# Fourier mixing after top-k attention on one core: the token tails folded once, on GpSimd, and the row sums' small constant added by ScalarE

## The chip, the cores and the metric

The kernel runs on one core of a Trainium2 chip. The core has a matrix engine (TensorE, PE in the profile; its weight loads are a row of their own, PEld), a vector engine (VectorE, DVE), an activation engine (ScalarE, ACT), a general engine (GpSimd, POOL) and queues that start transfers (SyncE, SP). Each engine works through its own list of instructions in order and waits at semaphores for the others. The metric is the device time of one execution, in microseconds (us), as the median of several runs.

## The reference

There are 8 batches. Each has 8 heads, 576 tokens and 64 channels per head. What is computed, per batch:

```
scores = q k^T / 8                       # 576 x 576 per head
kth    = 32nd largest score of each row
attn   = exp(scores - max) where scores >= kth, else 0
attn   = attn / (row sum + 1e-9)
x      = attn v, heads side by side       # 576 x 512
mixed  = Re FFT over channels (FFT over tokens (x))
u      = x + mixed
un     = (u - mean) / sqrt(var + 1e-6)
out    = u + relu(un w_ch1) w_ch2         # 512 -> 2048 -> 512
```

All of it is float32.

## The kernel before, in words

**Attention.** A batch has 4 pairs of heads, and a pair has 9 items (line 265): four token tiles of 128 rows for each of two heads, and one item for the remaining 64 tokens of both heads. So a batch is 36 items and the kernel 288. The 576 tokens are two halves of 288 = 128 + 128 + 32; tiles 0 and 1 are the first half's full tiles, 2 and 3 the second's, and tile 4 holds the two tails of 32, the first half's in partitions 0 to 31 and the second half's in 32 to 63.

For an item, TensorE makes the scores (lines 298, 313, 328), ScalarE moves them out of PSUM, and VectorE finds the 32 largest with four rounds of `max` and three of `match_replace` (lines 349, 351). GpSimd then makes two bounds per row from them (`bounds`, line 358, tile `nt`), ScalarE a mask term (line 365), GpSimd subtracts it (line 366), ScalarE takes the exponential and sums each row into `den` (line 372), TensorE transposes the result (line 393) and multiplies it with `v` (line 430). `attended` (line 439) copies the product out, moves two pieces of `den`, and leaves on a list for VectorE the function `inverse`: add 1e-9 (line 457), take the reciprocal (line 460), result in `rd`. `to_tokens` (line 465) transposes the product back into rows of tokens and scales it by `rd` into `x` (line 479, or on ScalarE at line 498 for batch 1).

**Fourier mixing.** The transform over tokens uses symmetries so that its matmuls are shorter. First the input is folded. Over tokens: a token and the one 288 later are added (even frequencies, parity 0) or subtracted (odd, parity 1). Over channels: the two halves of the 512 channels are added and subtracted, and within each result mirrored channels are added and subtracted. `fold_ops` (line 519) builds these operations for one batch and parity: `moved` brings the second half's tail down to partitions 0 to 31 (ScalarE, line 546), `first` is the token step (tile `sd`, line 551 for the full tiles and 554 for the tail), `second` the channel halves (tile `zw`, line 560), `third` the mirrored channels in two parts (tile `fg`, lines 569 to 581). Each step has a part for the two full tiles (128 partitions, two slots) and one for the tail (32 partitions, third slot). `dft_tokens` (line 603) then runs 30 matmuls per parity against tables of cosines and sines (line 617): 16 with the full tiles, 6 for one single channel, 8 with the tails. `dft_channels` (line 661) transforms over channels; the sum, the statistics and a reciprocal square root follow, partly on GpSimd (lines 696, 720 to 725), and the result is transposed for the network (line 737).

**Network.** `mlp_units` (line 745) cuts a batch's two matrix products into units: `hidden` (line 759), then `back` (lines 783, 819). They stand in a queue and are used as filler for TensorE.

**Order.** It is written out by hand. The main loop (line 1056) goes through steps; step i works on item i's top-k, on the scores of item i+3 and on the transposes of item i-2. `at(step, where, fn)` (line 889) puts a function at a place in a step: `pe` and its relatives among TensorE's work, `act` on ScalarE after the mask, `pool0` on GpSimd ahead of `bounds(i)`, `pool` after it, `dve` behind the step's top-k on VectorE. How much filler a step takes is settled by a planner from fixed costs (`fixed_cost`, `level`), not from measured times. The loop over batches at line 952 places each batch's folds, transforms and network: batch 0 ends with nothing behind it, and VectorE folds it whole (lines 957 to 966); for batch 1, GpSimd does `first` and `third` of the full tiles and VectorE the rest (lines 967 to 980); batches 2 to 6 are folded on GpSimd (lines 981 to 987); for the last batch VectorE folds parity 0 and GpSimd parity 1 at the same time (lines 988 to 994).

**Buffers.** The pool `batp` has one buffer per tag. `fold_s` holds in turn `sd`, `fg`, the moved mixed values of three tiles, the network's input and its output; `fold_d` holds `zw` and others.

Of the kernel before, what the change touches and what calls it, by code (L numbers as in the profile page):

```python
# [9 lines left out]
F32 = mybir.dt.float32  # L10
# [3 lines left out]
ALU = mybir.AluOpType  # L14
# [4 lines left out]
P = 128  # L19
# [40 lines left out]
def kernel(  # L60
# [378 lines left out]
    def attended(pair, ch, late):  # L439

        o, w = o_of.pop((pair, ch)), CW[ch]
        PT.pop((pair, ch))
        xT = attp.tile([P, CW[0]], F32, name=f"xT_{pair}_{ch}", tag="xT", bufs=4)
        nc.scalar.copy(out=xT[:, 0:w], in_=o[:, 0:w])
        xT_of[pair, ch] = xT
        den = den_t[pair % 3]
        if ch == 0:
            for h in range(2):
                nc.scalar.copy(
                    out=den[TH * h:TH * (h + 1), 5:6],  # L450
                    in_=den[TAIL + TH * h:TAIL + TH * (h + 1), 4:5],
                )
        c0, n = (0, 6) if ch == 0 else (6, 4)
        rd = small.tile([P, 6], F32, name=f"rd_{pair}_{ch}", tag="rd", bufs=6)

        def inverse():
            nc.vector.tensor_scalar(
                out=rd[:, 0:n], in0=den[:, c0:c0 + n], scalar1=1e-9, scalar2=None, op0=ALU.add
            )
# [56 lines left out]
    PARTS = [(slice(0, P), slice(0, 2)), (slice(0, TH), slice(2, 3))]  # L516
    folded, y_of, yt_of, us_of, rs_of, unT_of = ({} for _ in range(6))

    def fold_ops(b, par, eng, space="own", mid=None):

# [4 lines left out]

        def buf(n, name):  # L530
            if space == "hT":
                return sp[:, 3 * DM * n:3 * DM * (n + 1)].rearrange("p (s c) -> p s c", s=3)
            pool, tag = (batp, ("fold_s", "fold_d")) if space == "own" else (attp, ("PT0", "PT1"))
            return pool.tile([P, 3, DM], F32, name=f"{name}_{b}_{par}", tag=tag[n % 2], bufs=1)

        got = folded[b, par] = []

        def place(n):
            while len(got) <= n:
                got.append(buf(len(got), ("sd", "zw", "fg")[len(got)]))  # L540
            return got[n]

        def moved():

            out, in_ = place(0)[0:TH, 2, :], x[TH:TAIL, 4, :]
            nc.scalar.copy(out=out, in_=in_)

        def first(p):
            sd, op = place(0), ALU.add if par == 0 else ALU.subtract
            if p == 0:  # L550
                eng[0].tensor_tensor(out=sd[:, 0:2, :], in0=x[:, 0:2, :], in1=x[:, 2:4, :], op=op)
            else:
                s_ = sd[0:TH, 2, :]
                eng[1].tensor_tensor(out=s_, in0=x[0:TH, 4, :], in1=s_, op=op)

        def second(p):
            pp, ss = PARTS[p]
            s_, z_ = place(0)[pp, ss], place(1)[pp, ss]
            for cols, op in ((slice(0, Q2), ALU.add), (slice(Q2, DM), ALU.subtract)):
                (mid or eng[p]).tensor_tensor(  # L560
                    out=z_[:, :, cols], in0=s_[:, :, 0:Q2], in1=s_[:, :, Q2:DM], op=op
                )

        def third(n, p):
            pp, ss = PARTS[p]
            z_, f_ = place(1)[pp, ss], place(2)[pp, ss]

            def tt(out, up, down, op):
                eng[p].tensor_tensor(out=f_[:, :, out], in0=z_[:, :, up], in1=z_[:, :, down], op=op)

            if n == 0:
                eng[p].memset(f_[:, :, Q1:Q1 + 1], 0.0)
                eng[p].tensor_copy(out=f_[:, :, 0:DM:Q2], in_=z_[:, :, 0:DM:Q2])
                up, down = slice(1, Q1), slice(Q2 - 1, Q1, -1)
                tt(up, up, down, ALU.add)
                tt(slice(Q1 + 1, Q2), up, down, ALU.subtract)
            else:
                up, down = slice(Q2 + 1, Q3), slice(DM - 1, Q3, -1)
                tt(up, up, down, ALU.subtract)
                tt(slice(Q3, DM - 1), up, down, ALU.add)  # L580
                eng[p].tensor_copy(out=f_[:, :, DM - 1:DM], in_=z_[:, :, Q3:Q3 + 1])

        return {"moved": moved, "first": first, "second": second, "third": third}

    def fold_steps(f, moved=True):

        def one():
            if moved:
                f["moved"]()
            f["first"](0)  # L590
            f["first"](1)

        def two():
            f["second"](0)
            f["second"](1)

        def three(n):
            f["third"](n, 0)
            f["third"](n, 1)

        return [one, two, lambda: three(0), lambda: three(1)]

    def dft_tokens(b, par):

        while any(u[2] == "hidden" for u in queue):
            one_unit()
        _, zw, fg = folded[b, par]
        if b not in y_of:
            y_of[b] = batp.tile([P, 4, S], F32, name=f"y_{b}", tag="y")
        y = y_of[b]  # L610
# [17 lines left out]
        for g2 in range(2):  # L628
            for gg in range(2):
                g = 2 * g2 + gg  # L630
                for st in range(2):
# [29 lines left out]
    def dft_channels(b, t, quick=False):  # L661
# [22 lines left out]
        key = (b, t > 1 and t < 4)  # L684
        if key not in us_of:
            us_of[key] = batp.tile(
                [P, 3, DM], F32, name=f"us_{b}_{t}", tag="fold_d" if key[1] else "fold_s"
            )
        us = us_of[key][0:rows, CHUNKS[int(key[1])].index(t), :]
        nc.scalar.copy(out=two(us), in_=mp[0:rows])  # L690
# [261 lines left out]
    for b in range(B):  # L952
# [3 lines left out]
        T0 = end + (2 if first else 3 if soon else 4)  # L956
        if first:

            def folds(b=b, T0=T0):
                for par, space in ((0, "own"), (1, "hT")):  # L960
                    f = fold_ops(b, par, (nc.vector,) * 2, space)
                    at(T0, "act", f["moved"])
                    for op in fold_steps(f, False):
                        at(T0, "dve", op)
            at(T0, "begin", folds)
            ft, fc = (T0 + 1, T0 + 1), T0 + 1
        elif soon:
# [12 lines left out]
            ft, fc = (T0 + 3, T0 + 6), T0 + 7  # L980
        elif not last:
            for par in range(2):
                def folds(par=par, b=b, T0=T0):
                    for n, op in enumerate(fold_steps(fold_ops(b, par, (nc.gpsimd,) * 2))):
                        at(T0 + (6 if par else 1) + n, "pool0", op)
                at(T0, "begin", folds)
            ft, fc = (T0 + 5, T0 + 11), T0 + 12
        else:
            def folds(b=b):
                a = fold_steps(fold_ops(b, 0, (nc.vector,) * 2))  # L990
                for op in a + fold_steps(fold_ops(b, 1, (nc.gpsimd,) * 2, "PT")):
                    op()
            at(T0, "dve", folds)
            ft, fc = (T0 + 1, T0 + 3), T0 + 4
# [207 lines left out]
```

## Time and profile before

The median of three runs is 2008.23 us (2002.4 to 2011.8). The profiled execution spans 2002.2 us at a mean granted TensorE clock of 0.966.

| engine | busy us | share of the span |
|---|---|---|
| TensorE, matmuls | 1856.8 | 93% |
| VectorE | 1639.2 | 82% |
| ScalarE | 1230.1 | 61% |
| GpSimd | 835.0 | 42% |

The groups of instructions that the change touches, by line and shape:

| line, engine, operation | shape | count | busy us | mean ns |
|---|---|---|---|---|
| 457 VectorE, add 1e-9 | 128x4 | 32 | 14.0 | 437 |
| 457 VectorE, add 1e-9 | 128x6 | 32 | 10.6 | 332 |
| 546 ScalarE, move the tail | 32x512 | 15 | 9.2 | 617 |
| 551 GpSimd, token step | 128x1024 | 13 | 31.2 | 2398 |
| 554 GpSimd, token step, tail | 32x512 | 11 | 14.3 | 1302 |
| 560 GpSimd, channel halves | 128x512 | 22 | 28.5 | 1314 |
| 560 GpSimd, channel halves, tail | 32x256 | 22 | 16.1 | 749 |
| 569 GpSimd, mirrored channels | 128x254 | 52 | 37.8 | 749 |
| 569 GpSimd, mirrored channels, tail | 32x127 | 44 | 19.0 | 449 |
| 560 VectorE, channel halves | 128x512 | 8 | 7.2 | 942 |

The page cuts the span into 40 slices of 50 us and gives each engine's busy share in each; it is read first for which engine is full where. An average over the span hides that the first batch, the middle and the end have different limits. A group's busy time counts from an instruction's start to its end, so an instruction that is held up after its start looks long. "Idle before" is the time in which an engine stood still ahead of an instruction, with the instruction that released it.

### The profile page before, as it was taken

The numbers are of one execution on the slowest core, as the hardware profiler recorded it, in microseconds if no ns is written. First come the engines' busy times: TensorE is split into PE (matmuls) and PEld (weight loads), VectorE is DVE, ScalarE is ACT, GpSimd is POOL, SyncE is SP. The second block draws the span as 40 slices with busy tenths as digits, with TensorE's granted clock in tenths as the row PEclk, the third lists the DMA queues.
The fourth block names the chain that finished last, engine by engine and source line by source line (L and its number), as shares of the span: only waits on it lengthen the run. The fifth ranks groups of instructions, "written<-read, shape, count | busy, mean of one in ns | idle before, by whom it ended". The sixth has DMA issues, their size and how long they took to land.

```text
span 2002.2 us, 27534 instructions
## 1 busy us (share of the span) xinstructions
PE 1856.8 (93%) x8626; PEld 1122.8 (56%) x8626; DVE 1639.2 (82%) x3391; ACT 1230.1 (61%) x3047; POOL 835.0 (42%) x1114
## 2 busy tenths in 40 slices
PE   5666589999889999999999999999999999998999
PEld 3333356475555656647565656646565656565655
DVE  7999989999999999988889888888889889843100
ACT  6888747776766767656676667656665667541100
POOL 4878833324433365224632374225533464223000
PEclk9777699999999999999999999999999999998999
DMA  4333100011000100000000001010000101000000
GB/s 123 102 84 100 56 5 19 24 27 31 17 19 24 27 24 24 19 23 21 24 24 18 24 15 29 19 32 19 18 24 24 26 13 30 1 14 1 11 14 11
DMA packets 133585, 57.82 MB, mean 29 GB/s; under 512 B 124352, under 2 KB 124480, under 8 KB 133440
## 3 DMA queue, kind: packets, MB, share of 16 engines
q1 hardware_dynamic: 132208, 55.73, 10.5%
q8 instruction: 69, 1.13, 0.2%
q14 instruction: 76, 0.62, 0.1%
q10 hardware_dynamic: 1232, 0.33, 0.1%
HBM read 46.57 MB, written 9.44 MB: 28 GB/s over the span
## 4 chain that ended last, share of the span: by engine, by line
PE 70%; DVE 12%; issue 6%; ACT 6%; POOL 6%; DMA 0%; POOLq 0%; DVEq 0%; ACTq 0%
PE cp L783 20%; PE hp L759 19%; PE o L430 7%; PE sp L328 5%; PE tpP L393 5%; DVE m L349 5%; DVE wk L351 4%; PE yp L617 3%; POOL wk L366 2%; PE cp L819 2%; PE mp L673 2%; PE sp_t L298 2%; ACT wk L365 1%; ACT wk L372 1%; POOL w L192 1%
## 5 line engine op out<-in xcount | busy, mean ns | idle before, releaser
L366 POOL TENSOR_TENSOR wk<-S,wk 128x576 f32<-128x576 f32 x288 | 409.9, 1423 | 861.8 <-ACT wk L365 814.0
L349 DVE MAX8 m<-wk 128x8 f32<-128x576 f32 x864 | 623.1, 749 | 5.4
L759 PE MATMUL hp<-unT,w 128*128 128x256 f32 (+1 forms) x2048 | 538.0, 409 | 3.7 <-POOL t L721 2.2
L783 PE MATMUL cp<-w,hT 128*128 128x512 f32 x1024 | 478.7, 599 | 0.0
L759 PEld LDWEIGHTS hp<-unT,w 128*128 128x128 f32 x2048 | 372.5, 190 | 128.0 <-issue 32.0
L351 DVE MATCH_REPLACE8 wk<-m,wk 128x576 f32<-128x576 f32 x576 | 427.6, 742 | 0.0
L783 PEld LDWEIGHTS cp<-w,hT 128*128 128x128 f32 x1024 | 179.5, 190 | 183.1 <-issue 182.3
L372 ACT ACTIVATE wk<-wk,nt 128x576 f32<-128x576 f32 x288 | 224.9, 781 | 76.5 <-POOL wk L366 75.1
L393 PE MATMUL tpP<-ident,wk 128*128 128x128 f32 x1152 | 189.0, 289 | 74.7 <-ACT wk L372 39.0
L365 ACT ACTIVATE wk<-S,nt 128x576 f32<-128x576 f32 x288 | 226.2, 785 | 48.2 <-POOL nt L358 46.0
L393 PEld LDWEIGHTS tpP<-ident,wk 128*128 128x128 f32 x1152 | 141.4, 147 | 177.9 <-ACT wk L372 61.3
L349 DVE MAX8 m<-S 128x8 f32<-128x576 f32 x288 | 214.1, 743 | 30.4 <-ACT S L302 29.9
L396 ACT COPY PT<-tpP 128x512 f32<-128x512 f32 (+1 forms) x320 | 171.0, 545 | 109.5 <-PE tpP L393 107.1
L763 ACT ACTIVATE hT<-hp 128x320 f32<-128x320 f32 (+1 forms) x256 | 104.8, 409 | 188.7 <-PE hp L759 186.8
L351 DVE MATCH_REPLACE8 wk<-m,S 128x576 f32<-128x576 f32 x288 | 213.7, 742 | 0.0
L430 PE MATMUL o<-PT,v 128*64 128x256 f32 (+3 forms) x1440 | 194.5, 413 | 4.9 <-ACT PT L396 4.4
L331 ACT COPY S<-sp 128x512 f32<-128x512 f32 (+1 forms) x264 | 141.9, 588 | 73.0 <-PE sp L328 72.7
L328 PE MATMUL sp<-kT,qT 64*128 64x512 f32 (+1 forms) x528 | 166.5, 689 | 2.9 <-ACT means L937 1.9
L430 PEld LDWEIGHTS o<-PT,v 128*64 128x64 f32 x1440 | 110.9, 152 | 78.2 <-issue 15.7
L192 POOL TENSOR_TENSOR w<-w,space 128x512 f32<-128x512 f32 x96 | 123.6, 1287 | 5.3 <-ACT space L183 2.0
L797 DVE SCALAR_TENSOR_TENSOR x<-cp,gi,x 128x512 f32<-128x512 f32 x11 | 8.2, 746 | 128.3 <-PE cp L783 128.3
L298 PEld LDWEIGHTS sp_t<-kt,qT 128*128 128x128 f32 (+1 forms) x322 | 51.7, 188 | 62.6 <-issue 23.8
(123 smaller groups left out, 1874.4 us busy)
## 6 DMA issues: line engine op xcount, KB each, us to landing
space<-in_moe_w_ch_dram SPq DMA_DIRECT2D x32, 512.0 KB, 3.7
nat<-in_q_dram SPq DMA_DIRECT2D x128, 64.0 KB, 2.1
v<-in_v_dram SPq DMA_DIRECT2D x128, 64.0 KB, 2.2
out_dram<-x SPq DMA_DIRECT2D x32, 256.0 KB, 2.1
nat<-in_k_dram SPq DMA_DIRECT2D x124, 64.0 KB, 2.2
nat<-in_q_dram SPq DMA_DIRECT2D x128, 8.0 KB, 1.8
v<-in_v_dram SPq DMA_DIRECT2D x128, 8.0 KB, 1.8
nat<-in_k_dram SPq DMA_DIRECT2D x124, 8.0 KB, 1.7
```

The lines of the kernel that those rows point to most:

```text
L192: nc.gpsimd.tensor_tensor(out=dst, in0=dst, in1=(low, high, ex)[part], op=ALU.mult if part else ALU.add,)
L328: nc.tensor.matmul(sp[r], lhsT=qT[hd, q_cols], rhs=kT[hd, :], start=True, stop=True)
L349: ops.append(lambda src=src, m8=m8: nc.vector.max(out=m8, in_=src))
L351: ops.append(lambda src=src, m8=m8: nc.vector.match_replace(w, m8, src, NEG))
L365: nc.scalar.activation(out=w, in_=Ssb[i], func=AF.Relu, scale=-FAR, bias=Nt[i][:, 1:2])
L366: nc.gpsimd.tensor_tensor(out=w, in0=Ssb.pop(i), in1=w, op=ALU.subtract)
L372: nc.scalar.activation(out=w, in_=w, func=AF.Exp, bias=Nt.pop(i)[:, 0:1], accum_out=den_t[pair % 3][:, c:c + 1],)
L393: nc.tensor.transpose(tp[:, c, :], p_sb[:, k0 + P * c:k0 + P * (c + 1)], ident)
L396: nc.scalar.copy(out=pt[:, NF * he:NF * (he + 1), col:col + w], in_=tp[:, :, o:o + w])
L430: nc.tensor.matmul(o[D * e:D * (e + 1), c0:c1], lhsT=vv[:, c, e, :], rhs=pt[:, 2 * NF if c == NF else NF * e + c, c0:c1], start=(c == 0), ...
L759: nc.tensor.matmul(hp[:, 0:w], lhsT=w1[:, dt, P * it:P * (it + 1)], rhs=unT[:, dt, 0:w], start=(dt == 0), stop=(dt == NDT - 1),)
L783: nc.tensor.matmul(cp, lhsT=hT[:, it, P * n:P * (n + 1)], rhs=w2[:, it, :], start=(it == 0), stop=(it == NIT - 1),)
```

## The change

There are three parts.

1. The tails are no longer folded over tokens. All 64 rows of tile 4 are folded over channels only, once per batch, by GpSimd (`fold_tails`), into a tile of their own (`fold_t`, with one more column for the single channel). Both parities use it: the tables for the tail rows are now made for the tokens' own positions, for 64 rows. `moved` and the tail parts of `first`, `second` and `third` are gone. `fold_tails` is placed one step ahead of the folds (for batch 0 behind the bounds of that step, for the others ahead of them).
2. Batch 1's folds are all on GpSimd: `first` and `second` in one step, both parts of `third` in the next, for each parity.
3. `inverse` is now only the reciprocal on VectorE. ScalarE adds the 1e-9, in `attended`, behind the copies of `den`.

```diff
-            a = 2.0 * np.pi * ((np.outer(P * st + p, kk) % S) / S)
+            tok = P * st + p
+            if st == 2:
+                tok = np.where(p < TH, tok, S // 2 + tok - TH)
+            a = 2.0 * np.pi * ((np.outer(tok, kk) % S) / S)
...
-        def inverse():
-            nc.vector.tensor_scalar(
-                out=rd[:, 0:n], in0=den[:, c0:c0 + n], scalar1=1e-9, scalar2=None, op0=ALU.add
-            )
-            nc.vector.reciprocal(out=rd[:, 0:n], in_=rd[:, 0:n])
-
-        late.append(inverse)
+        nc.scalar.activation(out=rd[:, 0:n], in_=den[:, c0:c0 + n], func=AF.Copy, bias=1e-9)
+        late.append(lambda: nc.vector.reciprocal(out=rd[:, 0:n], in_=rd[:, 0:n]))
...
-    ROWS3 = (P, P, TH)
+    ROWS3 = (P, P, TAIL)
...
+    def fold_tails(b, eng):
+        z = batp.tile([P, DM], F32, name=f"zt_{b}", tag="fold_s")[0:TAIL]
+        ft_of[b] = batp.tile([P, DM + 1], F32, name=f"ft_{b}", tag="fold_t")
+        f = ft_of[b][0:TAIL]
+        fold_halves(eng, x_of[b][0:TAIL, 4, :], z)
+        for n in range(2):
+            fold_channels(eng, z, f[:, 0:DM], n)
+        eng.tensor_copy(out=f[:, DM:DM + 1], in_=z[:, Q1:Q1 + 1])
...
-        for st in range(3):
+        for st in range(2):
             mm(0, 1, st, zw[:, st, Q1:Q1 + 1], 1, 0)
+        mm(0, 1, 2, tails[:, DM:DM + 1], 1, 0)
...
-                mm(g2, gg, 2, fg[:, 2, P * g:P * (g + 1)], P, gg)
+                mm(g2, gg, 2, tails[:, P * g:P * (g + 1)], P, gg)
...
         if first:
-            def folds(b=b, T0=T0):
+            at(T0 - 1, "pool", lambda b=b: fold_tails(b, nc.gpsimd))
+            def folds(b=b):
                 for par, space in ((0, "own"), (1, "hT")):
-                    f = fold_ops(b, par, (nc.vector,) * 2, space)
-                    at(T0, "act", f["moved"])
-                    for op in fold_steps(f, False):
-                        at(T0, "dve", op)
-            at(T0, "begin", folds)
+                    for op in fold_ops(b, par, nc.vector, space):
+                        op()
+            at(T0, "dve", folds)
         elif soon:
+            at(T0 - 1, "pool0", lambda b=b: fold_tails(b, nc.gpsimd))
             for par in range(2):
-                def folds(par=par, b=b, T1=T0 + 1 + 3 * par):
-                    f = fold_ops(b, par, (nc.gpsimd, nc.vector), mid=nc.vector)
-                    at(T1 if par else T1 - 1, "act", f["moved"])
-                    at(T1, "pool0", lambda: f["first"](0))
-                    at(T1, "dve", lambda: [
-                        f["first"](1), f["second"](0), f["second"](1),
-                        f["third"](0, 1), f["third"](1, 1),
-                    ])
-                    at(T1 + 1, "pool0", lambda: [f["third"](n, 0) for n in range(2)])
+                def folds(par=par, b=b, T0=T0):
+                    for n, op in enumerate(fold_ops(b, par, nc.gpsimd)):
+                        at(T0 + 1 + 3 * par + n // 2, "pool0", op)
                 at(T0, "begin", folds)
         elif not last:
+            at(T0, "pool0", lambda b=b: fold_tails(b, nc.gpsimd))
             for par in range(2):
                 def folds(par=par, b=b, T0=T0):
-                    for n, op in enumerate(fold_steps(fold_ops(b, par, (nc.gpsimd,) * 2))):
+                    for n, op in enumerate(fold_ops(b, par, nc.gpsimd)):
                         at(T0 + (6 if par else 1) + n, "pool0", op)
         else:
+            at(T0 - 1, "pool0", lambda b=b: fold_tails(b, nc.gpsimd))
             def folds(b=b):
-                a = fold_steps(fold_ops(b, 0, (nc.vector,) * 2))
-                for op in a + fold_steps(fold_ops(b, 1, (nc.gpsimd,) * 2, "PT")):
+                a = fold_ops(b, 0, nc.vector)
+                for op in a + fold_ops(b, 1, nc.gpsimd, "PT"):
                     op()
```

More of the change, by code (lines that the diff above doesn't have):

```diff
@@ L514, with fold_channels, tt, fold_halves @@
     Q1, Q2, Q3 = DM // 4, DM // 2, 3 * DM // 4
-    ROWS3 = (P, P, TH)
-    PARTS = [(slice(0, P), slice(0, 2)), (slice(0, TH), slice(2, 3))]
-    folded, y_of, yt_of, us_of, rs_of, unT_of = ({} for _ in range(6))
-    def fold_ops(b, par, eng, space="own", mid=None):
+    ROWS3 = (P, P, TAIL)
+    folded, ft_of, y_of, yt_of, us_of, rs_of, unT_of = ({} for _ in range(7))
+    def fold_channels(eng, z, f, n):
+        def tt(out, up, down, op):
+            eng.tensor_tensor(out=f[..., out], in0=z[..., up], in1=z[..., down], op=op)
+        if n == 0:
+            eng.memset(f[..., Q1:Q1 + 1], 0.0)
+            eng.tensor_copy(out=f[..., 0:DM:Q2], in_=z[..., 0:DM:Q2])
+            up, down = slice(1, Q1), slice(Q2 - 1, Q1, -1)
+            tt(up, up, down, ALU.add)
+            tt(slice(Q1 + 1, Q2), up, down, ALU.subtract)
+        else:
+            up, down = slice(Q2 + 1, Q3), slice(DM - 1, Q3, -1)
+            tt(up, up, down, ALU.subtract)
+            tt(slice(Q3, DM - 1), up, down, ALU.add)
+            eng.tensor_copy(out=f[..., DM - 1:DM], in_=z[..., Q3:Q3 + 1])
+    def fold_halves(eng, s_, z):
+        for cols, op in ((slice(0, Q2), ALU.add), (slice(Q2, DM), ALU.subtract)):
+            eng.tensor_tensor(out=z[..., cols], in0=s_[..., 0:Q2], in1=s_[..., Q2:DM], op=op)
+    def fold_tails(b, eng):
[6 more added lines that the diff above has]
+        eng.tensor_copy(out=f[:, DM:DM + 1], in_=z[:, Q1:Q1 + 1])
+    def fold_ops(b, par, eng, space="own"):
         x = x_of[b]
@@ L531, in buf @@
             if space == "hT":
-                return sp[:, 3 * DM * n:3 * DM * (n + 1)].rearrange("p (s c) -> p s c", s=3)
+                return sp[:, 2 * DM * n:2 * DM * (n + 1)].rearrange("p (s c) -> p s c", s=2)
             pool, tag = (batp, ("fold_s", "fold_d")) if space == "own" else (attp, ("PT0", "PT1"))
-            return pool.tile([P, 3, DM], F32, name=f"{name}_{b}_{par}", tag=tag[n % 2], bufs=1)
+            return pool.tile([P, 2, DM], F32, name=f"{name}_{b}_{par}", tag=tag[n % 2], bufs=1)
@@ L536, in fold_ops @@
         got = folded[b, par] = []
[L538 to L569, printed above, removed]
-            if n == 0:
[L572 to L601, printed above, removed]
+        def first():
+            got.append(buf(0, "sd"))
+            op = ALU.add if par == 0 else ALU.subtract
+            eng.tensor_tensor(out=got[0], in0=x[:, 0:2, :], in1=x[:, 2:4, :], op=op)
@@ L603, in dft_tokens, with second, third @@
+        def second():
+            got.append(buf(1, "zw"))
+            fold_halves(eng, got[0], got[1])
+        def third(n):
+            if n == 0:
+                got.append(buf(2, "fg"))
+            fold_channels(eng, got[1], got[2], n)
+        return [first, second, lambda: third(0), lambda: third(1)]
     def dft_tokens(b, par):
@@ L607, in dft_tokens @@
         _, zw, fg = folded[b, par]
+        tails = ft_of[b]
         if b not in y_of:
@@ L686, in dft_channels @@
             us_of[key] = batp.tile(
-                [P, 3, DM], F32, name=f"us_{b}_{t}", tag="fold_d" if key[1] else "fold_s"
+                [P, 2 if key[1] else 3, DM], F32, name=f"us_{b}_{t}", tag="fold_d" if key[1] else "fold_s"
             )
```

## The prediction

> **What bounds the kernel now.** I read the page first: the shares of busy time, then the 40 slices.
>
> ```profile
> PE 1856.8 (93%) x8626; PEld 1122.8 (56%) x8626; DVE 1639.2 (82%) x3391; ACT 1230.1 (61%) x3047; POOL 835.0 (42%) x1114
> PE   5666589999889999999999999999999999998999
> DVE  7999989999999999988889888888889889843100
> ```
>
> TensorE (PE) is full from slice 6 on, except in slices 10 and 11 and in slice 36. VectorE (DVE) is full before that. The time is thus not "93% TensorE": it is a first stretch (batch 0's attention, nothing behind it) that VectorE sets, then a stretch where both are full, then one that TensorE sets. The table of busy time by 50 us windows gives the edges (columns: window, then busy us of PE, PEld, DVE, ACT, POOL, granted clock, DMA).
>
> ```profile
> 100.00:150.00 50.00, 30.84 (x143) 18.95 (x144) 49.45 (x101) 40.14 (x91) 36.58 (x36) 0.74 0.30 83
> 500.00:550.00 50.00, 41.97 (x233) 27.16 (x232) 49.44 (x103) 35.40 (x92) 24.46 (x29) 0.97 0.07 18
> 550.00:600.00 50.00, 43.75 (x213) 27.94 (x211) 48.42 (x105) 31.19 (x80) 15.76 (x33) 0.93 0.08 19
> 1100.00:1150.00 50.00, 50.00 (x258) 31.43 (x256) 43.06 (x90) 32.16 (x80) 16.96 (x19) 1.00 0.08 22
> 1800.00:1850.00 50.00, 40.17 (x174) 27.17 (x172) 17.97 (x24) 7.86 (x23) 15.86 (x20) 0.90 0.00 1
> ```
>
> From these: from 50 to 200 us VectorE has under 0.6 us idle in each 50, so what leaves VectorE leaves the time. From 500 to 600 TensorE idles 8.0 + 6.3 = 14.3 us while VectorE has 2.1 us idle in 100: there VectorE sets the pace, and this is where batch 1 is folded and transformed. From 800 to 1800 the same table leaves TensorE 6.6 us idle in 1000: nothing on VectorE, GpSimd (POOL) or ScalarE (ACT) is worth anything there. From 1800 to 1850 TensorE idles 9.8 us: batch 7's folds. So four places: A (0 to 257), B (257 to 290), C (480 to 600), E (1811 to 1832).
>
> The instructions that the change touches, in those places. First the row-sum step, all 64 (min/median/max ns), then batch 1's first parity in VectorE's timeline (start us, duration us, idle before):
>
> ```profile
> L457 DVE TENSOR_SCALAR rd<-den x64: 157/161/1308, 64.7 to 1792.1; 128x6 f32<-128x6 f32 x32, 128x4 f32<-128x4 f32 x32
> ```
> ```profile
> 488.24 1.43 DVE L554 TENSOR_TENSOR sd<-x,sd 32x512 f32<-32x512 f32 x1
> 491.92 3.16 DVE L560 TENSOR_TENSOR zw<-sd 128x512 f32<-128x512 f32 x4 [2.25 <-POOL sd L551]
> 495.20 1.93 DVE L569 TENSOR_TENSOR fg<-zw 32x127 f32<-32x127 f32 x4
> ```
>
> A four-element add that takes 157 ns at best and 1308 at worst isn't computing: it waits for something. In the second fence VectorE stands 2.25 us for GpSimd's `sd` and is back at its top-k only at 497.12: 8.9 us from 488.24. The second parity takes 512.23 to 517.92, 5.7 us. What that does to TensorE, with batch 0 (271.15) for comparison:
>
> ```profile
> 271.15 7.15 PE L617 MATMUL yp<-fs,fsp 128*128 128x145 f32 x30 [1.91 <-DVE fsp L569]
> 510.29 0.66 PE L393 MATMUL tpP<-ident,wk 128*128 128x128 f32 x4 [1.95 <-ACT wk L372]
> 517.11 3.03 PE L617 MATMUL yp<-fs,fg 128*128 128x145 f32 x16 [2.26 <-POOL fg L569]
> 564.07 1.12 PE L393 MATMUL tpP<-ident,wk 128*128 128x128 f32 x4 [5.60 <-ACT kT L257]
> ```
>
> Last, batch 7: VectorE folds one parity, GpSimd the other, TensorE waits.
>
> ```profile
> 1811.76 3.40 DVE L551 TENSOR_TENSOR sd<-x 128x1024 f32<-128x1024 f32 x1
> 1815.09 1.74 DVE L554 TENSOR_TENSOR sd<-x,sd 32x512 f32<-32x512 f32 x1
> 1816.76 5.13 DVE L560 TENSOR_TENSOR zw<-sd 128x512 f32<-128x512 f32 x4
> ```
> ```profile
> 1823.12 2.27 PE L617 MATMUL yp<-fs,fg 128*128 128x145 f32 x8 [8.48 <-DVE fg L569]
> ```
>
> **What the Trainium skill says.** "SBUF — State Buffer", section "Who interferes with whom": VectorE and GpSimd share a port pair as an exclusive lock, taken by VectorE's copies and tensor_scalars in a two-port mode and by its operations with two SBUF inputs, and the loser stands for the whole instruction. The trace agrees: the add above ranges from 157 to 1308 ns, and `sd` takes VectorE 1203 ns at 265.8 and 3404 at 1811.8, where GpSimd's 2350 ns `sd` began 20 ns before it. MAX8 (743 to 749 ns mean) shows none of it, so folds on GpSimd don't slow the top-k. "GPSIMD Engine Reference", section 3.1: a tensor_tensor takes GpSimd 1.96 times as long; here 128x512 takes 1314 ns on GpSimd and 672 on VectorE alone. "TensorE: Matmul & The Clock Gate", section "What's actually happening": an idle window of about 3.4 us halves the clock. Here the granted clock is 0.50 from 272 to 276, 562 to 566 and 1822 to 1830, each beside an idle stretch of TensorE, though at 271 that was only 1.91 us. "ScalarE: Activation LUTs", section "Table sets": cheap functions such as copy are in every set, so a Copy with a bias should load no table; the page has one table load in all, with Copy and Exp mixed.
>
> **The change part by part.**
>
> Row sums. 64 VectorE adds (24.6 us busy in all) become 64 ScalarE activations. In A there are eight, 4.45 us together by the busy time of that line from 0 to 260. ScalarE issues each just behind the copies of `den` it already makes; the nearest row, a 32x1 copy there, takes 189 ns. Where the reciprocal waits for ScalarE already (238 us, 0.64 us) about 0.2 of the gain is lost. Each reciprocal (177 to 193 ns over all 64) shows no lock. **A: 4.0 us** (3.5 to 4.5). After 260 the line has 9.5 us up to 760, which helps C only as a lead, and 10.7 us later, hidden behind full TensorE. ScalarE gains 64 x 0.19 = 12.2 us and loses the 16 `moved` copies of 0.617 = 9.9; it is 61% busy, and I put the difference at nothing.
>
> Tails, batch 0. Off VectorE per parity: one 32x512 (1.35, then 0.67), two 32x256 (0.405 each), four 32x127 (0.27), two small copies and a memset (0.34), and once the 1.43 us wait for the moved tail: 5.0 + 2.9 = 7.9 us of the 15.6 from 257.45 to 273.04; call it 7. GpSimd gets them once, for 64 rows: the nearest rows are 32-row ones, 2 x 0.749 + 4 x 0.449 + 0.09 + 0.19 + 2 x 0.18 = 3.9 us. They are queued a step earlier, behind the bound at 251.06; GpSimd stands idle from there to 259.50, so `fold_s` is free again (about 255.2) before VectorE wants it at 257.4. TensorE reaches the first transform at 264.90 by its own order (masks, scores, a mean), so that one doesn't move. The second no longer waits 1.91 us, and its 30 matmuls need 4.28 us, as at 727 in the chain, rather than 7.15 at half clock. **B: 4 us**, from 1.9 (the clock stays halved) to 4.8.
>
> Batch 1. VectorE loses 8.9 + 5.7 = 14.6 us in a stretch where it is the bound. GpSimd gets, per parity, 2.37 (`sd`) + 2 x 1.31 = 5.0 us in one step and 4 x 0.75 + 0.5 = 3.5 in the next, against 2.4 and 3.5 now, and 3.9 of tails two steps earlier. All of it stands ahead of the bound `nt` of that step on GpSimd's queue; ScalarE's mask waits for `nt`, and behind the mask in ScalarE's order stand the evacuations that TensorE needs. I lay GpSimd out from 489.09: `sd` to 491.5, halves to 494.1, `nt` 494.3 (now 492.0); mask, subtract to 496.6; thirds to 500.1, `nt` 500.3 (now 500.7, held by VectorE); next subtract to 502.6; `nt` 502.8 (now 505.8); subtract to 505.1 (now 508.7); second parity to 510.1, subtract to 512.6, thirds to 516.1 (now 519.3). So for one step GpSimd is 2.3 us later than VectorE was, then it is earlier, 3.2 us by the second transform. From there VectorE has its lead and TensorE can fill: idle after 520 is 1.9 + 1.1 + 2.2 + 4.1 = 9.3 us by the 10 us windows, of which the gap at 564 keeps perhaps 2 (GpSimd's 4.4 us of rsqrt stays ahead of the subtract there). 3.2 + 7.3, and half a microsecond from half-clock time: **C: 11 us**, from 2 to 17 (all 14.3 and the clock's loss).
>
> Batches 2 to 6. GpSimd's tails were 5.0 us per parity, 10.0; they are 3.9 now and one step earlier. Full TensorE hides it: **0**, bounds -2 and +2 by the idle there.
>
> Batch 7. The tails go to GpSimd a step ahead, in its idle stretch from 1791.05 to 1811.74. VectorE's start of the first matmul group loses 1.67 (the 32x512) and two of the four halves (5.13 / 2 = 2.56), together 4.2, of which I keep 3.6, for the two engines then alternate on the lock at other points. The second group (0.88 idle now) follows without a gap: 4.5, and some clock. **E: 5 us**, from 2 to 8 (half-rate matmuls after 1823 cost about 3 more).
>
> TensorE's own work: the tail matmuls read 64 rows instead of 32; 128-row and 32-row ones of that line take 295 and 303 ns, so nothing. Buffers: `fold_d` shrinks by a third, the tail's output takes it.
>
> Sum: 4 + 4 + 11 + 0 + 5 = 24 us of the span, 2002.2, so a span of 1978. That profiled run is the low end of the three times (2002.4, 2008.2, 2011.8); against the median: 2008.2 - 24 = **1984**.
>
> **The rivals.**
>
> GpSimd takes VectorE's place in batch 1. For it: 6.6 us of GpSimd per fold step against about 5.3 of top-k, with `nt` behind it, and ScalarE already stood 5.35 us for `nt` once at 500.9. Against: my layout, where it is later in one step only. Then C gives 1 and the rest 13: 1994.
>
> TensorE is the bound throughout and the lead isn't used. For it: its order is fixed in advance, with the same filler in each step, and from 290 to 500 both engines are full. Against: the idle of 14.3 us sits just behind the folds. Then A and E alone, in part: 8 us, 2000.
>
> Slower: the tails step stalls each batch. 3.9 us of GpSimd stand one step earlier, ahead of `nt`, in seven batches. If each came through to TensorE, and batch 1's four fold steps lost 3 us each: 27 + 12 - 13 = +26, 2034. It decides if a step's GpSimd work (1.41 + 3.9 + 0.19, and about 0.9 for the mask between) exceeds TensorE's step of 222 / 36 = 6.2 us: it is 6.4, but with two steps of slack in the buffers. Against it: a 3.86 us piece stands at the same place now, at 1151.5, and TensorE is busy 49.5 us of the 50 there.
>
> **How the numbers follow.** Forecast 66%, GpSimd in place of VectorE 16%, unused lead 11%, slower 7%. No change means within 0.5%, 10 us, about what this measurement can tell. The forecast falls within 10 us in 2 of its 66; the GpSimd case is faster in 12 of 16, else the same; the unused lead is the same, in 1 of 11 faster: faster 0.77, same 0.16, slower 0.07. The low end: all upper bounds, 4.5 + 4.8 + 17 + 8 = 34, gives 1974, less some 6 for the scatter of runs: 1968. The high end takes in the second and third cases: 2002.
>
> **What would show it.** Right: no line on VectorE but `max` and `match_replace` from 486 to 520; TensorE's idle from 500 to 600 down from 14 to about 5 us; the second transform of batch 0 without a wait and at full clock; TensorE's gap at batch 7's folds near 5 us rather than 8.5; 64 short ScalarE operations near 190 ns. Wrong: ScalarE's waits for `nt` growing at batch 1's folds, VectorE waiting for GpSimd's use of `fold_s`, or TensorE's idle between 800 and 1800 above 10 us.

## The result, and the profile after

The changed kernel takes 1980.54 us (median of five, 1978.57 to 1980.87), the one before 2006.94 (median of five, 2002.4 to 2011.8): a ratio of 0.9867, interval 0.9847 to 0.9887. Executions of the kernel before lie mostly near 2003 or near 2011 us, so its median moves with the draw (2003.4 to 2004.3 in three later series of 7 to 23, against which 23 to 24 us are won), and the profiled one is of the faster group. The forecast was 1984 within 1968 to 2002. The two profiled executions span 2002.2 and 1976.8 us, 25.4 apart, against a forecast sum of 24. The sum is right; two of its terms aren't, and these two offset each other.

First the page of the changed kernel, the same three lines as before.

```profile
PE 1849.8 (94%) x8626; PEld 1120.5 (57%) x8626; DVE 1595.5 (81%) x3273; ACT 1223.6 (62%) x3095; POOL 813.2 (41%) x1088
PE   5666599999999999999999999999999999998999
DVE  7999989999899999988889888988889888853000
```

VectorE lost 43.7 us of busy time and TensorE's two weak slices (10 and 11) are full. TensorE's own busy time also fell by 7.0 us with the same 8626 matmuls, in part because fewer of them ran at half clock. The 50 us windows (busy us of PE, PEld, DVE, ACT, POOL, clock, DMA):

```profile
150.00:200.00 50.00, 30.99 (x157) 18.85 (x153) 47.33 (x94) 41.06 (x94) 45.10 (x42) 0.77 0.31 92
500.00:550.00 50.00, 45.33 (x250) 30.50 (x250) 46.51 (x102) 36.46 (x96) 31.24 (x49) 0.97 0.06 16
550.00:600.00 50.00, 50.00 (x244) 31.24 (x241) 48.95 (x100) 35.05 (x91) 14.09 (x18) 1.00 0.08 19
```

TensorE's idle from 500 to 600 went from 14.3 us to 4.7. From 150 to 200 VectorE now has 2.7 us idle, where it had almost none: in batch 0's stage it was relieved, and waits.

Busy shares don't say when the time was won. For that I take GpSimd's 288 bounds `nt`, one per item and in the same order in both kernels, as marks, and read the time between the same marks in both traces (start of the item's bound; differences worked out from the timelines before rounding):

| stretch | before | after | won | forecast |
|---|---|---|---|---|
| start to item 0 | 20.3 | 19.3 | 1.0 | 0 |
| items 0 to 36, batch 0's attention (A) | 230.8 | 230.1 | 0.7 | 4 |
| items 36 to 72, batch 0's folds and transform (B) | 221.2 | 218.1 | 3.1 | 4 |
| items 72 to 96, batch 1's folds and transform (C) | 148.3 | 137.0 | 11.2 | 11 |
| items 96 to 284, batches 2 to 6 | 1143.7 | 1138.9 | 4.8 | 0 |
| item 284 to the end, batch 7 (E) | 238.0 | 233.3 | 4.6 | 5 |

Nothing was changed ahead of item 0, and a kernel with the old folds (`rs_only` below) has 19.5 there, so the first row is scatter. Batch 0's stretch scatters too: seven kernels with the same code there, the changed one and six of the experiments, take 229.5 to 232.7, 231.2 on average, and the two traces with the adds on VectorE (the kernel before and `rs_dve`) take 230.8 each. So the 0.7 us in that row can't be told from nothing. The wins in C and from 96 to 284 are clear: kernels that share their code there agree within 0.1 us. The last stretch varies by up to 0.8 us between such kernels. For B and the last stretch, the other kernel with the old folds (`rs_only`) takes 3.3 and 2.5 us more than the kernel before, so those two wins are known against one trace only.

In B, the second parity's matmuls no longer stand behind a fold and run at full clock (TensorE's timeline: start us, duration us):

```profile
267.52 2.83 PE L598 MATMUL yp<-fs,fsp 128*128 128x145 f32 x20
```

Before, it was 7.15 us with a gap of 1.91 ahead. The 20 here are the full tiles' and the single channel's; the ten with the tails' rows follow at 270.28. By the first matmul of `dft_channels` (271.88, before 278.32) 4.75 us are won since item 36. Then 1.7 us are lost again, for a gap that both kernels have a little later meets a different clock (before, then after):

```profile
291.66 4.54 PE L759 MATMUL hp<-unT,w 128*128 128x320 f32 x16 [2.17 <-POOL t L721]
285.12 6.26 PE L741 MATMUL hp<-unT,w 128*128 128x320 f32 x16 [2.08 <-ACT unT L722]
```

Before, the granted clock stays at 1.00 from 288 to 300; in the changed kernel it is 0.50 from 286 to 288 and 0.69 from 288 to 290. So half clock didn't go from B: it fell on 16 later matmuls, in the traces of the changed kernel and of all its edits (6.24 to 6.27 us), and B won 3.1 us rather than 4.8.

In C, GpSimd does what was laid out for it in the first parity. Its timeline, second step and bound of item 75, then TensorE's remaining gaps:

```profile
486.69 2.51 POOL L537 TENSOR_TENSOR zw<-sd 128x512 f32<-128x512 f32 x2
489.16 0.19 POOL L363 TENSOR_TENSOR nt<-m,cc 128x2 f32<-128x2 f32 x1
```
```profile
504.27 1.11 PE L398 MATMUL tpP<-ident,wk 128*128 128x128 f32 x4 [2.22 <-ACT wk L377]
511.56 2.94 PE L598 MATMUL yp<-fs,fg 128*128 128x145 f32 x16 [1.11 <-POOL fg L521]
```

With the 4.8 us already won subtracted, the layout of the prediction put that bound at 489.5; it came at 489.16. The second parity came later than laid out, for GpSimd had to wait for ScalarE's mask:

```profile
501.91 1.41 POOL L371 TENSOR_TENSOR wk<-S,wk 128x576 f32<-128x576 f32 x1 [4.63 <-PE tpP_t L413]
```

Its thirds end at 513.7, where the layout, less the same 4.8, has 511.3. So by the second transform (511.56, before 517.11) only 0.8 of the 3.2 us foreseen had been won; the rest came behind it. The gap of 5.60 us before a later transpose is gone from the timeline.

In E, VectorE's timeline and the first matmul:

```profile
1790.95 3.41 DVE L570 TENSOR_TENSOR sd<-x 128x1024 f32<-128x1024 f32 x1
1794.39 3.30 DVE L537 TENSOR_TENSOR zw<-sd 128x512 f32<-128x512 f32 x2
1798.36 2.99 DVE L521 TENSOR_TENSOR fg<-zw 128x254 f32<-128x254 f32 x4
1798.92 4.21 PE L598 MATMUL yp<-fs,fg 128*128 128x145 f32 x16 [5.09 <-DVE fg L521]
```

The gap fell from 8.48 to 5.09 us, and the second group no longer waits. The 16 matmuls take 4.21 us where the same 16 take 2.25 at 263: half clock is still paid (the granted clock is 0.50 from 1798.9 to 1803). VectorE's `sd` still takes 3.41 us, for GpSimd's begins 30 ns earlier.

### The profile page after: what moved, and what is told of

Same layout as the page of the kernel before. It is cut to its first block, busy times and chain, and to the rows that moved or that the text cites. A ratio compares the mean times of both kernels' runs of the same rounds, so it can differ in the third digit from the quotient of the medians.

```text
span 1976.8 us, 27373 instructions
## 1 busy us (share of the span) xinstructions
PE 1849.8 (94%) x8626; PEld 1120.5 (57%) x8626; DVE 1595.5 (81%) x3273; ACT 1223.6 (62%) x3095; POOL 813.2 (41%) x1088
## 4 chain that ended last, share of the span: by engine, by line
PE 82%; DVE 6%; ACT 5%; POOL 4%; issue 2%; SPq 0%; DMA 0%; POOLq 0%; DVEq 0%; ACTq 0%
PE hp L741 24%; PE cp L765 22%; PE o L435 8%; PE sp L333 6%; PE tpP L398 6%; PE yp L598 3%; PE cp L801 3%; DVE m L354 3%; PE mp L655 2%; DVE wk L356 2%; PE sp_t L303 2%; POOL wk L371 2%; POOL w L197 1%; ACT wk L377 1%; PE tpk L252 1%
## 5 line engine op out<-in xcount | busy, mean ns | idle before, releaser
L333 PE MATMUL sp<-kT,qT 64*128 64x512 f32 (+1 forms) x528 | 162.3, 675 | 2.4 <-ACT means L919 1.9
L435 PEld LDWEIGHTS o<-PT,v 128*64 128x64 f32 x1440 | 111.4, 153 | 79.1 <-issue 17.4
```

Source lines behind the costliest of these rows:

```text
L333: nc.tensor.matmul(sp[r], lhsT=qT[hd, q_cols], rhs=kT[hd, :], start=True, stop=True)
L435: nc.tensor.matmul(o[D * e:D * (e + 1), c0:c1], lhsT=vv[:, c, e, :], rhs=pt[:, 2 * NF if c == NF else NF * e + c, c0:c1], start=(c == 0), ...
```

## The experiments

All are edits of the changed kernel, except `rs_only`. The stretches are those of the table; times are medians where runs were timed.

**Row sums back on VectorE (`rs_dve`).**

```diff
-        nc.scalar.activation(out=rd[:, 0:n], in_=den[:, c0:c0 + n], func=AF.Copy, bias=1e-9)
-        late.append(lambda: nc.vector.reciprocal(out=rd[:, 0:n], in_=rd[:, 0:n]))
+        def inverse():
+            nc.vector.tensor_scalar(
+                out=rd[:, 0:n], in0=den[:, c0:c0 + n], scalar1=1e-9, scalar2=None, op0=ALU.add)
+            nc.vector.reciprocal(out=rd[:, 0:n], in_=rd[:, 0:n])
+        late.append(inverse)
```

> The changed kernel with the 1e-9 added by VectorE again (64 adds), all else kept. Marks are GpSimd's bounds of items 0, 36, 72, 96 and 284; from 0 to 36 they take 230.1 us in the changed kernel and 230.8 in the one before. Theory 1 (the prediction's step A: VectorE alone sets batch 0's stage): the adds cost what they last, 3.5 to 4.5 us from item 0 to 36, so some 234. Theory 2 (from the two traces: once VectorE is relieved, masks, scores and weight loads stand close behind it, so only 0.7 us was won): item 0 to 36 takes 230.5 to 231.5, and the rest of the span changes by under 1.5 us; in all 1 to 2 us slower than the changed kernel.

Items 0 to 36 take 230.8 us, 0.7 more than in the changed kernel; 0.9 more from 96 to 284, 0.7 more in batch 7. Time: 1980.91 us against 1980.54. That is theory 2: part 3 of the change is worth a microsecond or two at most, below what these times tell apart. Of the marks, the 0.9 us is the one that stands clear of scatter.

**Part 3 alone (`rs_only`):** the same edit the other way round, in the kernel before.

> The kernel before with part 3 alone: ScalarE adds the 1e-9, folds as they were. Theory 1 (step A as predicted): 4 us won from item 0 to 36 and perhaps 1 to 2 us more up to item 96, 2002 for a span before of 2002.2 becomes 1996 to 1998. Theory 2 (other limits stand close behind VectorE there): 0.7 us won from item 0 to 36, 0 to 2 us over the rest.

Items 0 to 36 take 230.6 us (230.8 before): theory 2 there. But the whole is not faster: 2008.06 us, ratio 1.0012 with interval 1.0004 to 1.0021, which neither theory expected. The marks put it in two places: 224.6 us against 221.2 in B and 240.4 against 238.0 in batch 7. In both, TensorE's gap is the same as before (1.91, and 8.49 against 8.48 us), but half clock lasts longer after it. In B:

```profile
270.19 8.08 PE L612 MATMUL yp<-fs,fsp 128*128 128x145 f32 x30 [1.91 <-DVE fsp L564]
```

Here the 30 matmuls take 8.08 us (7.15 before), and the next 16 take 6.13 us, where they take 3.72 in the kernel before. By 10 us windows the clock is 0.50 from 270 to 280 and 0.84 from 280 to 290; before it was 0.66 and 1.00. The same gap cost 3.3 us more. Why the clock came back later isn't shown by anything here; with one trace of each kernel it may be a matter of the execution and not of the kernel.

**Needless work on VectorE in batch 0 (`vec_dummy`).**

```diff
...
+        if pair < NPB:
+            some_row = fs.rearrange("p a b c k -> p (a b c k)")[:, 0:S]
+            late.append(lambda: nc.vector.max(out=junk, in_=some_row))
```

> The changed kernel with one needless maximum of 576 elements on VectorE behind each of batch 0's eight reciprocals, 8 x 0.67 = 5.4 us of VectorE with no lock in it. Theory 1 (VectorE alone sets batch 0's stage): items 0 to 36 take 5.4 us longer, 235.5. Theory 2 (two limits close together, about 3 us of VectorE's lead is lost in waits there): part of it goes into those waits, 2 to 3.5 us longer, 232 to 233.5.

Items 0 to 36 take 231.4 us, 1.3 more than in the changed kernel and within the scatter of that stretch; 1979.16 us in all. The maxima cost VectorE less than planned: seven of the eight lie in this stretch, and its busy time there grows by 3.6 us, not 5.4. So theory 1 would mean about 3.6 us here, and the 1.3 found is less than even theory 2 expected. With a scatter of 3 us, one trace speaks against theory 1 but doesn't measure what is left of it. What speaks plainly is VectorE's share of the stretch, items 0 to 36 in the kernel before and in the changed one (columns as in the windows above):

```profile
20.31:251.06 230.75, 141.49 (x658) 86.11 (x655) 225.58 (x452) 187.33 (x413) 186.97 (x177) 0.76 0.30 88
19.30:249.37 230.07, 139.81 (x659) 85.60 (x659) 221.60 (x445) 187.36 (x421) 186.97 (x177) 0.74 0.30 89
```

VectorE has 4.0 us less to do and stands idle 3.3 us longer (8.5 us, before 5.2). VectorE's timeline tells where. Up to 148 us the lead that the missing adds give grows with each reciprocal: VectorE reaches the fourth at 144.57, the kernel before at 148.53, 4.0 us, of which 1.0 is from the start. In the kernel with the adds back, the same reciprocal is 0.88 early, and stays so to the end of the stage. In the changed kernel the lead then goes into waits (VectorE's timeline of the changed kernel):

```profile
166.18 0.76 DVE L354 MAX8 m<-S 128x8 f32<-128x576 f32 x1 [0.63 <-ACT S L307]
171.75 0.70 DVE L167 TENSOR_SCALAR wm<-space 128x512 int32<-128x512 int32 x1 [1.19 <-DMA nat<-in_q_dram]
179.16 0.69 DVE L167 TENSOR_SCALAR wm<-space 128x512 int32<-128x512 int32 x1 [0.36 <-ACT w L182]
```

By the seventh reciprocal it's 1.7 us. These are waits for scores, for a load (the operation held up is one on a weight chunk), and for ScalarE's conversion of a chunk. The other kernels with this code also reach the fourth reciprocal 3.2 to 4.1 us early and lose 1.3 to 3.5 us of it by the fifth: most of the stretch's scatter arises there.

**What stands behind VectorE there (`nojoin`, `nojoin_dummy`).** Two of GpSimd's three joins per weight chunk are left out, without and with the eight maxima.

```diff
-        at(s0 + 1, "pool", lambda n=n: join(n, (1, 2)))
```

> The changed kernel with two of GpSimd's three joins per weight chunk left out (64 operations of 1.29 us, 82 us of GpSimd in batch 0's stage; the weights then lack their exponent and sign). To be read beside nojoin_dummy. Theory 1 (GpSimd's joins, ahead of subtracts and next weight loads, are the second limit of batch 0's stage, close behind VectorE): items 0 to 36 shorten from 230 to 225 to 228 us, and no more, since VectorE then sets it. Theory 2 (the second limit is elsewhere, in ScalarE's or the loads' own time): 229.5 to 231.

> The same with the eight needless maxima on VectorE behind batch 0's reciprocals (5.4 us). With GpSimd's joins in place they cost under 1 us. Theory 1 (VectorE alone sets the stage once GpSimd is light): items 0 to 36 take 4.5 to 5.4 us more than in nojoin. Theory 2 (something else stands close behind VectorE still): 0 to 2.5 us more.

Without the joins items 0 to 36 take 225.9 us, 4.2 less and outside the scatter, and VectorE keeps its lead past 148 us (6.5 us at the seventh reciprocal). Its busy time is the same 221.6 us as with the joins, so the joins weren't slowing VectorE's own operations; only its idle time falls, from 8.5 to 4.3 us:

```profile
19.34:245.23 225.89, 142.34 (x658) 86.14 (x659) 221.57 (x446) 186.71 (x421) 107.59 (x113) 0.77 0.31 90
```

So the joins were the second limit, as theory 1 of `nojoin` says. Whether they act through the subtracts behind them or through the next weight loads isn't separated. With the maxima on top it is 227.2, 1.4 more, not 4.5 to 5.4; VectorE's busy time grows by 3.7 us and its idle time falls from 4.3 to 2.0. Taken as it stands, even then VectorE doesn't set the stage alone, but each of the two kernels has one execution, and the difference is smaller than the scatter of this stretch elsewhere. What else stands close behind VectorE is open.

**Batch 1's halves on VectorE again (`b1_mixed`).**

```diff
...
-                    for n, op in enumerate(fold_ops(b, par, nc.gpsimd)):
-                        at(T0 + 1 + 3 * par + n // 2, "pool0", op)
+                    for n, op in enumerate(fold_ops(b, par, nc.gpsimd, mid=nc.vector)):
+                        at(T0 + 1 + 3 * par + n // 2, "dve" if n == 1 else "pool0", op)
```

> The changed kernel, but batch 1's channel halves of the full tiles are done by VectorE again (behind its top-k, with a wait for GpSimd's first step); tails stay folded once on GpSimd. Items 72 to 96 take 137.0 us in the changed kernel and 148.3 before. Theory 1 (VectorE was the bound there, each microsecond it stands behind its top-k comes through): it holds VectorE for about 3.5 and 1.5 us, so 4 to 6 us come back, some 142. Theory 2 (GpSimd's latency ahead of the bounds is what costs now): it takes 2.6 us per parity off GpSimd's queue, so 136 to 138 or faster.

Items 72 to 96 take 140.3 us, 3.2 more than with everything on GpSimd and 8.0 less than before; 1982.21 us in all. Up to item 80 it is 1.3 us faster than the changed kernel, for GpSimd has less ahead of the bounds; then VectorE's holdups (it waits 3.09 and 1.30 us for `sd`, and works 2 x 1.29) come through and TensorE has a gap of 3.73 us at 551 again. Theory 1, a little smaller than expected. So of C's 11.2 us, 3.2 are the move to GpSimd; the other 8.0 came with the rest of the change, nearly all with the single fold of the tails (part 3 alone, `rs_only`, gives 0.6 in this stretch).

**Batch 0's tails on VectorE (`b0_tails_vec`).**

```diff
-            at(T0 - 1, "pool", lambda b=b: fold_tails(b, nc.gpsimd))
+            at(T0, "dve", lambda b=b: fold_tails(b, nc.vector))
```

> The changed kernel, but batch 0's tails are folded by VectorE, ahead of its other folds, rather than by GpSimd one step earlier. That puts about 2.6 us on VectorE at 255.6. Theory 1 (step B: what was won there is TensorE's wait for the second parity and the half clock after it): the second parity is ready at about 267.5, just when TensorE comes to it, so 0 to 1 us is lost up to item 72 and the clock stays at 1.0. Theory 2 (each microsecond on VectorE there counts): 2.6 us are lost.

Items 36 to 72 take 218.1 us, the same as in the changed kernel, and 1979.20 us in all. Theory 1 for the transform: B's win is that the second parity is ready when TensorE comes to it, and the few microseconds by which it is ready earlier are worth nothing.

**ScalarE's copies, and GpSimd's old tail work, put back in batches 2 to 6 (`act_copies`, `pool_pad`).**

```diff
...
+            for s in (T0 + 1, T0 + 6):                       # act_copies
+                at(s, "pool0", lambda b=b: nc.scalar.copy(
+                    out=ft_of[b][TAIL:TAIL + TH, 0:DM], in_=x_of[b][TH:TAIL, 4, :]))
...
+            for s in (T0 + 1, T0 + 6):                       # pool_pad
+                for n in range(4):
+                    at(s + n, "pool0", lambda b=b, n=n: pad(b, n))
```

> The changed kernel with ScalarE's two 32x512 copies per batch put back in batches 2 to 6 at the steps where the old folds had them; they write rows that nothing reads. The changed kernel wins 0.75 to 1.0 us per batch from item 96 to item 284 (4.8 us in all), where the prediction said 0. Theory 1 (ScalarE's moved copies stood ahead of evacuations that TensorE needs): the copies give back 3.5 to 5 us between items 96 and 284. Theory 2 (it is GpSimd's lighter folds that let the bounds come earlier): under 1 us comes back.

> The changed kernel with GpSimd given operations of the size of the old tail parts (32x512; two 32x256; two 32x127; two 32x127) in batches 2 to 6 at the old steps, writing rows that nothing reads; about 4.3 us per parity, 43 us of GpSimd in all. Theory 1 (ScalarE's copies were the cost in these batches): under 1 us between items 96 and 284. Theory 2 (GpSimd's tails, ahead of the bounds, were): 3.5 to 5 us come back there.

From item 96 to 284: 1140.5 us with the copies (1.6 of the 4.8 come back) and 1144.1 with GpSimd's operations (5.2 come back); in all, 1980.91 and 1984.58 us. GpSimd's work was the main cause, the copies a smaller one. The two don't add up to 4.8, and `pool_pad` overshoots: in this stretch GpSimd is busy 483 us before, 456 in the changed kernel and 502 here. The view of waits shows the chain, ScalarE's mask waiting for the bounds over the whole kernel (us in total, times, longest), in the kernel before, the changed one, and with GpSimd's work back:

```profile
ACT wk L365 <- POOL nt L358: 46.0, 36, 5.6
```
```profile
ACT wk L370 <- POOL nt L363: 18.7, 16, 3.8
```
```profile
ACT wk L370 <- POOL nt L363: 45.9, 34, 3.8
```

Between items 96 and 284 these waits are 23.9, 5.7 and 32.9 us. With the copies back they are 1.9, so the copies don't act through the bounds; they take ScalarE's own time.

**Batch 7 on VectorE alone (`b7_vec`).**

```diff
-                for op in a + fold_ops(b, 1, nc.gpsimd, "PT"):
+                for op in a + fold_ops(b, 1, nc.vector, "PT"):
```

> The changed kernel with both parities of batch 7 folded by VectorE, one after the other, GpSimd idle. In the changed kernel VectorE and GpSimd fold one parity each at the same time and TensorE waits 5.1 us for the first, then works at half clock to 1805. Theory 1 (the two block each other on the shared port; a lone VectorE does a parity in 4.5 us): TensorE's gap falls to under 1 us, the clock stays up, and 5 to 8 us are won, 1969 to 1972 of span; the second parity is ready at about 1800, before its transform at 1809. Theory 2 (VectorE is simply slow at it, GpSimd's share is needed): the gap stays near 5 us or the second transform waits, no gain or a loss of up to 4 us.

1972.78 us (1972.43 to 1973.38), ratio to the kernel before 0.9835, interval 0.9808 to 0.9863; the last stretch takes 225.9 us, 7.5 less. VectorE and TensorE at that place:

```profile
1793.20 1.23 DVE L570 TENSOR_TENSOR sd<-x 128x1024 f32<-128x1024 f32 x1
1794.46 1.29 DVE L537 TENSOR_TENSOR zw<-sd 128x512 f32<-128x512 f32 x2
1795.88 1.42 DVE L521 TENSOR_TENSOR fg<-zw 128x254 f32<-128x254 f32 x4
1796.43 2.22 PE L598 MATMUL yp<-fs,fg 128*128 128x145 f32 x16 [0.35 <-DVE fg L521]
```

The same operations take 1.23, 1.29 and 1.42 us instead of 3.41, 3.30 and 2.99; the gap is 0.35 us and the clock stays full. VectorE has done both parities by 1801.4, the second transform begins at 1809. GpSimd's help in parallel cost 7.5 us. This is the fastest version of this study.

**Batches 2 to 6: halves on VectorE, with the above (`halves_vec`).**

```diff
...
-                    for n, op in enumerate(fold_ops(b, par, nc.gpsimd)):
-                        at(T0 + (6 if par else 1) + n, "pool0", op)
+                    for n, op in enumerate(fold_ops(b, par, nc.gpsimd, mid=nc.vector)):
+                        at(T0 + (6 if par else 1) + n, "dve" if n == 1 else "pool0", op)
...
```

> The changed kernel with batch 7 folded by VectorE, as in b7_vec (1971.6 us of span), and in batches 2 to 6 the channel halves on VectorE behind its top-k rather than on GpSimd ahead of the bounds: 2.6 us per parity off GpSimd's queue. pool_pad showed that GpSimd's work ahead of the bounds costs TensorE about 0.8 to 1 us per batch. Theory 1 (less GpSimd work there wins the rest): another 0.3 to 0.6 us per batch between items 96 and 284, 2 to 3 us in all, about 1969. Theory 2 (what is left no longer reaches TensorE, or VectorE's wait for the first step delays its top-k): within 1 us, or up to 3 us slower.

1972.89 us, and items 96 to 284 take 1138.9 us, the same as in the changed kernel. Theory 2: after the change GpSimd's work in those batches no longer reaches TensorE (idle 7.2 us in that stretch in both kernels), and relieving it by another 2.6 us per parity wins nothing.

## Why the prediction was right or wrong, point by point

- **C, batch 1 (11 us, measured 11.2): right** in mechanism, and in part by luck in size. VectorE was the bound there, and `b1_mixed` shows that what holds it comes through. TensorE's remaining idle of 4.7 us is about the 5 that was named as its sign. The layout of GpSimd held for the first parity; for the second it was 2.4 us too early, so 0.8 us was won by the second transform instead of 3.2, and some 10.4 behind it instead of 7.8.
- **B, batch 0 (4 us, measured 3.1): right,** between its two ends. The gap went, and `b0_tails_vec` shows that readiness for the second transform is what counted. Half clock left the transform as forecast, 4.75 us by its end, but the 16 matmuls behind the next gap took 6.26 us instead of 4.54, which the prediction didn't have. GpSimd had freed `fold_s` at 253.2, before VectorE wanted it.
- **E, batch 7 (5 us, measured 4.6): right,** with the gap near the 5 us named. The exclusive lock between VectorE and GpSimd that the Trainium skill describes ("SBUF — State Buffer", "Who interferes with whom") carried that step, and `b7_vec` fits it best: without GpSimd's operations the same VectorE operations take 3.9 us, with them 9.7.
- **A, row sums (4.0 us, 3.5 to 4.5; measured 0.7, not to be told from nothing): wrong.** The step that failed is "what leaves VectorE leaves the time", drawn from 49.45 busy us in 50. The work did leave: VectorE's busy time fell by 4.0 us. But its idle time grew by 3.3, nearly all of it in waits after the fourth reciprocal, up to which 3 us had been won. A full engine is only a bound up to the next limit, and that stood close behind: `nojoin` shows GpSimd's weight joins to be one. The ScalarE operation itself was sized fairly (208 ns, against 189 from the nearest row).
- **Batches 2 to 6 (0, bounds -2 and +2; measured 4.8): wrong.** "Full TensorE hides it" failed. TensorE was 99% busy, but GpSimd's folds stood ahead of the bounds and ScalarE's mask waited for them; `pool_pad` shows that this reaches TensorE. The price was 0.8 to 1.5 us per batch, five times. TensorE's visible idle accounts for 3.2 of the 4.8 us (10.4 before, 7.2 after); the trace counts the rest as matmul time at full clock, and how it splits isn't shown.
- **The sum.** A was 3.3 us too high, batches 2 to 6 4.8 too low. The forecast of 24 was close to 25.4 partly because these offset.
- **The rivals.** GpSimd didn't take VectorE's place, though `b1_mixed` shows that its work ahead of the bounds costs 1.3 us up to item 80; and the lead was used where TensorE had gaps. ScalarE's waits for `nt` in C, named as a sign of being wrong if they grew, fell from 17.4 to 8.9 us. The slower case, a tails step that stalls each batch, had the right chain (GpSimd, bound, mask) with the wrong sign: some 5.5 us less GpSimd work per batch (27.6 in five) counted for more than its earlier place.

## What to carry to other kernels

Before an engine that is 99% busy is taken for the bound, ask how far behind it the next one stands: take a little work off it, or add some, and read whether its idle time or the stage's length moves, with the scatter of that stage from several traces beside it. Operations ahead of a small result that another engine waits for cost time even where the main engine looks full, for its gaps are short and many. Two engines that share a lock should not be given the same job at the same time when one of them alone would be done in time.

## What the runs showed of the hardware that was not expected

- The same TensorE gap had different prices. After 1.91 us of idle, half clock cost 3.3 us more in one trace than in another (16 matmuls that took 3.72 us took 6.13), and 2.5 us more after 8.5 us of idle at the end. A gap of 2.17 us at 291.66 brought no half clock where it had just been paid at 272 to 276 (the 16 matmuls behind it took 4.54 us); a gap of 2.08 us at 285.12, with full clock for over 30 us before it, did (6.26 us). What decides it isn't shown.
- Folding a parity takes VectorE 4.2 us alone (1793.20 to 1797.37) and 10.5 us (1790.95 to 1801.44) while GpSimd folds the other; GpSimd's own half operations go from 1.25 us each to 1.9.
